# Attention and gated MLP on one core: new measured costs in the instruction planner, and a new table of keys

## The chip, the cores and the metric

The kernel runs on 1 core of one Trainium2 chip. The metric is the device time in microseconds, the median of three runs. Short names: PE is TensorE (its matmuls; PEld its weight loads), DVE is VectorE, ACT is ScalarE, POOL is GpSimd, SP is SyncE, which issues all loads and stores.

## The reference, cut to what matters

q, k and v are 8 batches x 8 heads x 576 positions x 64. Heads 0 to 3 attend locally (a band of 32 positions), heads 4 to 7 along a stride of 32. The result x (576 x 512 a batch) goes through a gated MLP.

```python
scores = scale * np.matmul(q, k.transpose(0, 1, 3, 2))
mask_local = (rel >= 0) & (rel < stride)
mask_strided = (rel >= 0) & (pos[None, :] % stride == pos[:, None] % stride)
scores = np.where(masks[None, :, :, :], scores, -1000000000.0)
attn = np.exp(scores - np.max(scores, axis=-1, keepdims=True))
attn = attn / (np.sum(attn, axis=-1, keepdims=True) + 1e-09)
x = np.matmul(attn, v)                      # heads side by side: 512 wide
h = np.maximum(x @ w_in, 0.0)
u, v = (h[..., :d_ff // 2], h[..., d_ff // 2:])
v_n = (v - mu) / np.sqrt(var + 1e-06)       # over the last axis
v_s = np.einsum('ts,bsd->btd', w_spatial, v_n) + b_spatial[None, :, None]
return ((u * v_s) @ w_out).astype(np.float32)
```

## The kernel before, in words

Everything stays on the chip between the loads and the stores of the result. Each of the 8 batches has four attention tiles of two heads: tile t is `t % 4`, 0 and 1 local, 2 and 3 strided. An attention tile is: loads of q, k and v on SP; scores on PE (L494 local, 36 instructions, L637 strided, 32; each counts as two matmul records); for the first four tiles masks added by PE (L468) and a maximum on DVE (L514, L522, L662); exponentials on ACT (L551, L674); normalising (L447, L451, L456, L668) and a transposition (L575 local, L691 strided) on DVE into the single tile pc; copies of pc to ptl or pts by ACT and POOL (L399, L401); values on PE (L604 local, two halves, L708 strided) into two po buffers; and the split of each half into two fp32r parts, x: a cast on ACT (L421), which frees nothing yet, and the rest, po minus the cast, on DVE (L409), which frees the po buffer. Scores and values use small tiles of the array: 64x32, 128x32, 128x64 and 64x64 instead of 128x128.

The MLP uses full tiles, three fp32r products for each fp32 one: the v half (L969, 512 columns) and the u half (L1026, 288 columns) of w_in, the spatial product (L1107, with its tail L1119 and L1120), and the output projection by 7 block products (L1157), whose operands are split into tile g by a cast (L399 or L401) and a rest (L409). The weights w_in arrive as pairs of 32-bit words, and each of their eight parts is converted at the start by ACT (L789), POOL (L797) and DVE (L805) and then split into two (L399 or L401, L409), as the spatial weights wsp are (loaded in four parts).

All of this is written down as a list of operations, each with a key, the engines that may do it, its cost on each, and what it reads and writes. `Program.order` plans from that list: it goes through time, lets each engine take the ready operation of the lowest key, and gives an operation to another engine if it would end earlier there (`KEYS["dp"]` adds a handicap in ns for DVE, by kind of operation: kind 1 holds the two-input ones). On PE it counts a cost for changing between small-tile (`tiled`) and full-tile operations, and while it is in small tiles it prefers to stay there if the key of the next small tile is near enough. The order of the plan becomes the order of the instructions on each engine, and each engine then works strictly in that order. `KEYS` holds the numbers: "a" the due times of the first eight attention tiles, "lead" how much earlier than needed the later ones are due (10.96 before), "la" and "lb" when q, k and v are fetched, "wv", "wu", "s" and others the weights.

`fillers` looks at the plan: where PE would stand idle for over 700 ns ahead of an operation with a spare buffer (not the masked scores), it puts dummy matmuls of 256 columns there (L1385, `warm`), as many as 0.8 of the gap holds at 427 ns each, so that PE keeps working.

SP keeps at most eight loads under way: each load waits for the one eight places ahead of it. Buffers: two for q, two for k, two for v, two for po, one for pc.

## Time and profile before

| | us |
|---|---|
| runs | 508.29, 508.70, 509.73 |
| median | 508.70 |
| span of the profiled execution | 508.2 |
| PE busy in it | 495.6 |
| DVE, ACT, POOL busy | 345.7, 280.1, 111.4 |

The page gives the span of the profiled execution, from its first to its last instruction, as 508.2 us; the fastest run, 508.29, is the nearest to it. PE is busy for 98% of the span. A slice of 12.7 us near the start is the only one in which it does not reach nine tenths, beside the first and the last. The times of the page are to be read as starts and lengths; consecutive instructions of an engine overlap a little, so the distance between two starts is what an instruction takes of the engine's time.

### The profile page before, as it was taken

Reading aid. Unit: us, or ns where it says so; the run is one execution under the profiler, and the core shown is the slowest. Engines: PE = TensorE matmul, PEld = TensorE weight load, DVE = VectorE, ACT = ScalarE, POOL = GpSimd, SP = SyncE. Lnnn points to the kernel's source line nnn. Section 1 sums busy time; section 2 is a strip of 40 time slices with the busy share of each in tenths; the row PEclk is TensorE's granted clock in tenths of the full one; section 3 lists DMA queues with packets and bytes.
Section 4 is the critical chain, followed back from the end, with each engine's and each line's share of the span. In section 5 each row is a group of like instructions: output and inputs, shape, how many; then the busy total and the mean of one; then the engine's idle time right before and its main releaser. Section 6 shows DMA issues by size and latency. Waiting matters only on the chain.

```text
span 508.2 us, 15732 instructions
## 1 busy us (share of the span) xinstructions
PE 495.6 (98%) x6398; PEld 455.0 (90%) x6398; DVE 345.7 (68%) x1069; ACT 280.1 (55%) x871; POOL 111.4 (22%) x229
## 2 busy tenths in 40 slices
PE   7599999999999999999999999999999999999997
PEld 4478898889988999899998999989998899989997
DVE  3888898988678628784489935687288841666055
ACT  5797777677546566373644764355554642235214
POOL 3554325233232013120221211121022300120000
PEclk9599999999999999999999999999999999999999
DMA  8996442422423312305234243024231020002002
GB/s 288 402 342 233 124 149 98 137 93 56 152 90 121 126 50 91 86 26 153 81 92 138 72 135 91 2 90 135 63 99 44 0 95 0 1 2 93 1 1 94
DMA packets 26103, 52.69 MB, mean 104 GB/s; under 512 B 3120, under 2 KB 11440, under 8 KB 26032
## 3 DMA queue, kind: packets, MB, share of 16 engines
q1 hardware_dynamic: 26032, 51.70, 30.6%
q8 instruction: 50, 0.82, 0.7%
q14 instruction: 21, 0.17, 0.1%
HBM read 42.25 MB, written 9.44 MB: 102 GB/s over the span
## 4 chain that ended last, share of the span: by engine, by line
PE 93%; DMA 4%; DVE 1%; POOL 1%; SPq 0%; issue 0%; ACT 0%; POOLq 0%
PE m L1026 20%; PE m L1107 20%; PE m L969 20%; PE m L1157 18%; PE po L604 3%; PE po L708 3%; PE s L494 2%; PE s L637 2%; PE m L1119 2%; PE m L1120 2%; DMA vn<-w_in 2%; DMA x<-wsp 1%; DMA x<-wtail 1%; POOL ptl L401 0%; SPq L428 0%; POOL kbd L1321 0%
## 5 line engine op out<-in xcount | busy, mean ns | idle before, releaser
L1107 PE MATMUL m<-wsp_sb,vn 128*128 128x288 f32 x768 | 112.9, 296 | 0.0
L1107 PEld LDWEIGHTS m<-wsp_sb,vn 128*128 128x128 f32 x768 | 105.5, 189 | 0.9
L1026 PE MATMUL m<-x,w_in_sb 128*128 128x288 f32 x768 | 105.3, 297 | 0.0
L1026 PEld LDWEIGHTS m<-x,w_in_sb 128*128 128x128 f32 x768 | 103.0, 188 | 0.6
L969 PE MATMUL m<-w_in_sb,x 128*128 128x512 f32 (+1 forms) x408 | 99.5, 398 | 0.0
L1157 PE MATMUL m<-g,w_out 128*128 128x288 f32 x672 | 92.9, 296 | 0.0
L1157 PEld LDWEIGHTS m<-g,w_out 128*128 128x128 f32 x672 | 89.9, 188 | 1.3
L969 PEld LDWEIGHTS m<-w_in_sb,x 128*128 128x128 f32 (+1 forms) x408 | 74.1, 185 | 18.4
L401 POOL TENSOR_SCALAR ptl<-pc 32x64 f32<-32x64 f32 (+3 forms) x98 | 37.9, 387 | 107.2 <-DVE pc L575 71.5
L924 DVE BATCH_NORM_STATS2 bn<-vv 128x6 f32<-128x512 f32 (+1 forms) x37 | 25.3, 685 | 47.4 <-ACT vv L919 47.0
L399 ACT CAST g<-u 128x288 fp32r<-128x288 f32 x91 | 39.0, 435 | 29.1 <-DVE u L820 12.9
L551 ACT ACTIVATE pl<-pl,ml 128x64 f32<-128x64 f32 (+1 forms) x140 | 47.0, 337 | 7.8 <-DVE ml L531 7.7
L937 POOL TENSOR_TENSOR bn<-bn,sel 128x1 f32<-128x1 f32 (+1 forms) x37 | 21.5, 583 | 129.4 <-DVE bn L932 124.5
L409 DVE TENSOR_TENSOR g<-u,g 128x288 fp32r<-128x288 f32 x98 | 43.6, 459 | 7.6 <-ACT g L399 5.3
L919 ACT ACTIVATE vv<-m 128x512 f32<-128x512 f32 (+1 forms) x37 | 22.0, 596 | 47.2 <-PE m L969 46.9
L1129 DVE TENSOR_TENSOR u<-m,u 128x288 f32<-128x288 f32 x56 | 24.9, 454 | 30.6 <-PE m L1120 30.3
L1040 ACT ACTIVATE u<-m 128x288 f32<-128x288 f32 x56 | 22.9, 409 | 41.1 <-PE m L1026 40.3
L399 ACT COPY ptl<-pc 32x320 f32<-32x320 f32 (+3 forms) x94 | 33.5, 356 | 14.5 <-DVE pc L575 12.7
L421 ACT CAST x<-po 128x288 fp32r<-128x288 f32 x60 | 22.2, 399 | 22.1 <-PE po L604 10.6
L409 DVE TENSOR_TENSOR x<-po,x 128x288 fp32r<-128x288 f32 x64 | 27.3, 447 | 7.9 <-ACT x L421 7.1
L531 DVE CUSTOM_DVE_ANT_0 pl<-s,cst_sb 128x64 f32<-128x64 f32 (+1 forms) x140 | 22.1, 214 | 14.4 <-PE s L494 14.4
L551 ACT ACTIVATION_READ_ACCUMULATOR pl<-pl,ml 128x1 f32 (+1 forms) x140 | 26.4, 188 | 0.0
(128 smaller groups left out, 634.1 us busy)
## 6 DMA issues: line engine op xcount, KB each, us to landing
q<-qT SPq DMA_DIRECT2D x32, 295.0 KB, 4.1
v_raw<-vs SPq DMA_DIRECT2D x15, 512.0 KB, 3.7
v_raw<-vl SPq DMA_DIRECT2D x16, 384.0 KB, 3.5
k<-kT SPq DMA_DIRECT2D x16, 304.0 KB, 4.6
kbd<-ks SPq DMA_DIRECT2D x32, 144.0 KB, 4.8
outT<-o SPq DMA_DIRECT2D x32, 144.0 KB, 1.9
outT<-u SPq DMA_DIRECT2D x28, 144.0 KB, 1.8
vn<-w_in SPq DMA_DIRECT2D x4, 512.0 KB, 7.6
```

The lines of the kernel that those rows point to most:

```text
L399: eng.copy(dst(), src())
L401: eng.tensor_scalar(dst(), src(), 1.0, 0.0, op0=ALU.mult, op1=ALU.add)
L409: eng.tensor_tensor(dst(), src(), f32(hi()), op=ALU.subtract)
L421: eng.copy(dst(), src())
L551: eng.activation(p_sb()[:m, u, :], src, AF.Exp, bias=st()[:m, u : u + 1], scale=SCALE if masked else -1.0, **total,)
L924: lambda eng: eng.bn_stats(bn()[:m, 0:6], v()[:m]), [(v,)], [(bn,)],
L969: eng.matmul(v_ps()[:m, :], x_at(kt)[:, a, :], w_in_sb[:, w, kt, HF:], start=(n == 0 and i == 0), stop=(n == NT - 1 and i == 2),)
L1026: eng.matmul(u_ps()[:, :HS], w_in_sb[:, w, kt, f * P : (f + 1) * P], xs[NHP * b + kt]()[:, a, r], start=(n == 0 and i == 0), stop=(n == NT ...
L1040: lambda eng, u=u, f=f, u_ps=u_ps: eng.activation(flat(u)[:, f * HS : (f + 1) * HS], u_ps()[:, :HS], AF.Relu),
L1107: eng.matmul(s_ps()[:, :HS], vn()[:, a, kt, fs], wsp_sb[:, w, kt, r], start=(kt == 0 and i == 0), stop=False,)
L1129: lambda eng, ug=ug, s_ps=s_ps: eng.tensor_tensor(ug(), s_ps()[:, :HS], ug(), op=ALU.mult),
L1157: eng.matmul(o_ps()[:, :HS], w_out_t[0]()[:, w, r, BLOCKS[name], j * P : (j + 1) * P], at(a), start=(first and r == 0 and i == 0), stop=(r ...
```

## The change

The costs that the planner has for the four kinds of small tiles are replaced: local scores 936 to 905 ns, local values 588 to 585, strided scores 784 to 704, strided values 804 to 1066. The change between tile modes costs 88 ns on going into small tiles and nothing on leaving, where it was 45 ns each way. All of `KEYS` is new. The subtraction of "lead" moves from the list `when` to `due`, with the same result. The computation is the same.

```diff
-    "a": (-4467.57, -3072.23, -4097.95, -922.09, -62.58, 1948.86, -54.07, 1313.94,),
+    "a": (-14649.79, -11958.25, -12798.64, -3418.29, -1034.09, 2748.73, 22.98, 2612.65,),
...
-    "lead": (10.96,),
+    "lead": (6.61,),
...
-    "dp": (1410.82, -7913.25, 17481.82, 35293.8,),
+    "dp": (1728.09, 229.43, 40803.9, 48991.77,),
...
-                cost += 45.0 * ((n in self.tiled) != mode)
+                cost += 88.0 * (n in self.tiled and not mode)
...
-            due - 14, [(PE, 26 * 2 * S // STRIDE)], f_s, [(q,), *kin], [(p,) for p in s_ps],
+            due - 14, [(PE, 905)], f_s, [(q,), *kin], [(p,) for p in s_ps],
...
-                due - 1.5, [(PE, 6 * 98)], f_v, [*vin, *ptok], [(o_ps,)],
+                due - 1.5, [(PE, 585)], f_v, [*vin, *ptok], [(o_ps,)],
...
-            due - 14, [(PE, SB * 98)], f_s, [(q,), *kin], [(s_ps,)],
+            due - 14, [(PE, 704)], f_s, [(q,), *kin], [(s_ps,)],
...
-            due - 1.5, [(PE, 4 * SB * 22 + 100)], f_v,
+            due - 1.5, [(PE, 1066)], f_v,
...
-    when = [w - KEYS["lead"][0] for w in when]
...
-        return float(np.interp(t + 1, units, when))
+        return float(np.interp(t + 1, units, when)) - KEYS["lead"][0]
```

**The first values, on SP.** In the first 25 us SP loads the first tiles and the weights; q_2 is the query of tile 1, v_raw_0 the values of tile 0, vn, u and g here staging for w_in. Before:

```order
L428 DMA x_0_178<-wsp 128x576
L428 DMA v_raw_0_180<-vl 128x768
L428 DMA k_2_183<-kT 128x608
L428 DMA q_2_188<-qT 128x590
L428 DMA vn_0_101<-w_in 128x1024
L428 DMA xt_0_228<-vs 128x1024
L428 DMA vn_0_101<-w_in 128x1024
L428 DMA q_3_237<-qT 128x590
```

and after:

```order
L428 DMA q_2_186<-qT 128x590
L428 DMA g_1_188<-w_in 128x1024
L428 DMA x_0_180<-wsp 128x576
L428 DMA k_2_199<-kT 128x608
L428 DMA vn_0_97<-w_in 128x1024 x2
L428 DMA u_1_240<-w_in 128x1024
L428 DMA v_raw_0_243<-vl 128x768
L428 DMA q_3_250<-qT 128x590
```

The values of tile 0 stood two loads ahead of that query, as the 14th load, and now stand seven behind it, as the 22nd; the values of tile 2 (xt) moved ahead.

**The first values, on PE,** from the last scores of tile 1 (m_1, m_2) to the first work on x of tile 0 (x_3) or the values of tile 2 (po_2). Before:

```order
L494 MATMUL m_2_136<-k_1_106,q_2_188 32x64
L1385 MATMUL po_0_335<-zeros_67 32x256
L604 MATMUL po_0_335<-ptl_72,v_raw_0_180 64x96 x6
L604 MATMUL po_1_347<-ptl_72,v_raw_0_180 64x96 x6
L637 MATMUL m_3_139<-kbd_68,q_3_237 32x36 x32
L969 MATMUL m_4_406<-w_in_sb_62,x_3_354 128x512 x3
L708 MATMUL po_2_420<-pts_71,xt_0_228 64x2x18
```

and after:

```order
L494 MATMUL m_2_133<-k_1_176,q_2_186 32x64
L1384 MATMUL po_0_363<-zeros_67 32x256 x12
L604 MATMUL po_0_363<-ptl_72,v_raw_0_243 64x96 x6
L604 MATMUL po_1_385<-ptl_72,v_raw_0_243 64x96 x6
L637 MATMUL m_3_138<-kbd_68,q_3_250 32x36 x32
L708 MATMUL po_2_440<-pts_71,xt_0_136 64x2x18
```

One filler became twelve, and the values of tile 2 follow the scores of tile 3 without full matmuls between. The three fillers that stood ahead of the values of tile 1 are gone.

**The first x, on ACT:** the casts of x of tile 0 (x_3, from po_0 and po_1) and of tile 2 (x_5). Before:

```order
L421 CAST x_3_354<-po_0_335 128x288
L399 COPY pts_71<-pc_1_345 32x16x18
L421 CAST x_3_354<-po_1_347 128x288
L399 COPY pts_71<-pc_1_345 32x16x18
L551 ACTIVATE pl1_76,ml1_78<-m_1_133,ml1_78 128x64 x2
```

and after:

```order
L421 CAST x_3_392<-po_0_363 128x288
L789 ACTIVATE vn_0_97<-vn_0_97 128x512
L421 CAST x_3_392<-po_1_385 128x288
L789 ACTIVATE u_1_240<-u_1_240 128x512
L789 ACTIVATE vn_0_97<-vn_0_97 128x512
L789 ACTIVATE u_0_256<-u_0_256 128x512
L399 CAST w_in_sb_62<-w_out_0_191 128x512
L399 CAST wsp_sb_63<-x_1_128 128x576
L421 CAST x_5_494<-po_2_440 128x18x16
L421 CAST x_5_494<-po_3_442 128x18x16
```

Before, the exponentials of tile 1 (L551) came behind the casts of x of tile 0; now they stand ahead of them, and conversions of w_in stand around them.

**The steady part, on PE:** the end of the strided values of batch 2 and 3's tiles in the output projection, and what follows. Before:

```order
L708 MATMUL po_22_2127<-pts_71,v_raw_10_1878 64x2x18
L708 MATMUL po_23_2129<-pts_71,v_raw_10_1878 64x2x18
L1157 MATMUL m_44_2166<-g_7_1667,w_out_1_1208 128x288 x6
L494 MATMUL s_16_2180<-k_7_1473,q_13_1628 32x64
L494 MATMUL s_17_2182<-k_7_1473,q_13_1628 32x64
```

and after:

```order
L708 MATMUL po_28_2779<-pts_71,v_raw_13_2503 64x2x18
L708 MATMUL po_29_2781<-pts_71,v_raw_13_2503 64x2x18
L494 MATMUL s_20_2816<-k_8_2100,q_16_2512 32x64
L494 MATMUL s_21_2818<-k_8_2100,q_16_2512 32x64
```

Local scores now follow strided values directly. In the whole program POOL has 27 wide two-input operations that DVE had (fifteen of them L409 into g), where it had none.

## Rows read from the trace of the kernel before

**Rows 1.** The page, busy us, share and instructions of each engine.

```profile
PE 495.6 (98%) x6398; PEld 455.0 (90%) x6398; DVE 345.7 (68%) x1069; ACT 280.1 (55%) x871; POOL 111.4 (22%) x229
```

**Rows 2.** Waits of PE: line, for whom, us in total, times, longest.

```profile
PE m L494 <- DMA q<-qT: 7.3, 1, 7.3
```

**Rows 3.** Timeline of PE, start: start us, us, line, tiles, count.

```profile
17.76 1.34 PE L494 MATMUL m<-k,q 64*32 64x64 f32 x72 [7.28 <-DMA q<-qT]
19.03 1.06 PE L1385 MATMUL po<-zeros 128*32 128x256 f32 x2
20.02 2.19 PE L604 MATMUL po<-ptl,v_raw 128*64 128x96 f32 x24
...
30.65 1.48 PE L1385 MATMUL po<-zeros 128*32 128x256 f32 x6
...
43.77 2.40 PE L1026 MATMUL m<-x,w_in_sb 128*128 128x288 f32 x16
```

**Rows 4.** Windows: busy us of PE, PEld, DVE, ACT, POOL; PEclk, DMA, GB/s.

```profile
14.00:17.70 3.70, 0.00 (x0) 0.00 (x0) 3.67 (x10) 2.31 (x5) 0.63 (x1) 0.50 1.03 412
...
22.40:23.40 1.00, 0.95 (x65) 0.93 (x65) 0.71 (x3) 0.95 (x4) 0.30 (x1) 0.70 1.00 385
```

**Rows 5.** Chain of waits in order of time: start us, us, what.

```profile
466.17 12.81 PE m L1026 x96
```

**Rows 6.** Timeline of PE, one small-tile run in the steady part.

```profile
172.77 3.46 PE L1026 MATMUL m<-x,w_in_sb 128*128 128x288 f32 x24
176.16 0.97 PE L494 MATMUL s<-k,q 64*32 64x64 f32 x72
177.06 9.86 PE L1026 MATMUL m<-x,w_in_sb 128*128 128x288 f32 x72
```

**Rows 7.** Timeline of PE, scores followed by strided values.

```profile
54.43 0.97 PE L494 MATMUL s<-k,q 64*32 64x64 f32 x72
55.33 1.14 PE L708 MATMUL po<-pts,v_raw 64*64 64x36 f32 x64
56.40 0.67 PE L1107 MATMUL m<-wsp_sb,vn 128*128 128x288 f32 x3
```

**Rows 8.** Timeline of PE, scores followed by local values.

```profile
253.96 0.97 PE L494 MATMUL s<-k,q 64*32 64x64 f32 x72
255.00 1.21 PE L604 MATMUL po<-ptl,v_raw 128*64 128x96 f32 x24
```

**Rows 9.** DMA issues of 0 to 45 us: count, KB each, us to landing.

```profile
vn<-w_in SPq DMA_DIRECT2D x4, 512.0 KB, 7.6
...
k<-kT SPq DMA_DIRECT2D x5, 304.0 KB, 5.9
x<-wsp SPq DMA_DIRECT2D x4, 288.0 KB, 6.0
v_raw<-vl SPq DMA_DIRECT2D x3, 384.0 KB, 6.3
...
v_raw<-vs SPq DMA_DIRECT2D x2, 512.0 KB, 6.4
```

**Rows 10.** Timeline of DVE, the transposition of tile 0.

```profile
16.05 0.84 DVE L575 STREAM_TRANSPOSE pc<-pl 128x640 f32<-128x640 f32 x1
```

**Rows 11.** Timeline of ACT, exponentials and conversions.

```profile
23.13 0.31 ACT L551 ACTIVATE pl<-m,ml 128x64 f32<-128x64 f32 x1
...
23.44 0.30 ACT L551 ACTIVATE pl<-m,ml 128x64 f32<-128x64 f32 x1
...
27.52 1.27 ACT L789 ACTIVATE vn<-vn 128x512 f32<-128x512 f32 x2
```

**Rows 12.** Groups by line: count, busy us, mean ns, idle before.

```profile
L399 ACT CAST g<-u 128x288 fp32r<-128x288 f32 x91 | 39.0, 435 | 29.1 <-DVE u L820 12.9 <-PE m L1157 9.0 <-DVE u L1129 6.2
...
L409 DVE TENSOR_TENSOR g<-u,g 128x288 fp32r<-128x288 f32 x98 | 43.6, 459 | 7.6 <-ACT g L399 5.3 <-POOL g L401 1.6
...
L937 POOL TENSOR_TENSOR bn<-bn,sel 128x1 f32<-128x1 f32 x35 | 20.2, 580 | 127.0 <-DVE bn L932 122.1 <-DVE mx L447 4.6
```

More of the change, by code (lines that the diff above doesn't have):

```diff
@@ L41 @@
 KEYS = {
-    "a": (-4467.57, -3072.23, -4097.95, -922.09, -62.58, 1948.86, -54.07, 1313.94,),
-    "v": (-1905.33, 2566.85, -1420.01, -351.81,),
-    "u": (2077.2, 2507.69, 3441.61, -704.54,),
-    "s": (1600.35, 689.49, 1605.62, -2112.6,),
-    "t": (-863.37,),
-    "o": (2205.96, 3994.67,),
-    "cst": (-3153.23,),
-    "wv": (1302.43, 874.44, 1384.1, 1780.19,),
-    "wu": (-954.94, -624.77, 1601.45, 150.66,),
-    "lead": (10.96,),
-    "fill": (634.17, 3536.74, 3759.85, 2050.78, 1027.03, 2069.52,),
-    "dp": (1410.82, -7913.25, 17481.82, 35293.8,),
-    "dpt": (1128.82,),
-    "lv": (-2407.03, -1707.29, -454.82, -254.06,),
-    "lu": (1673.71, 2694.32, 1173.88, 457.25,),
-    "lo": (1682.63, -1711.68, 1604.3, -4779.41,),
-    "ls": (-1419.42, 1216.18, -2053.61, -239.17, 1173.72,),
-    "pre": (2.84, 55.65,),
-    "near": (3261.26,),
-    "la": (-2830.09, -2292.21, -5019.65, -1683.98, -4639.4, -3037.2, 298.54, 1600.86,),
-    "lb": (-1002.76, 2105.75, -428.93, 3194.59, 1811.71, 608.19, -588.14, 3548.95,),
+    "a": (-14649.79, -11958.25, -12798.64, -3418.29, -1034.09, 2748.73, 22.98, 2612.65,),
+    "v": (-22602.5, 6765.54, -8978.5, -1009.27,),
+    "u": (2367.68, 7294.49, 15422.81, -3910.53,),
+    "s": (-4960.75, 6447.03, 1975.51, -2850.99,),
+    "t": (4169.61,),
+    "o": (6420.48, 4905.57,),
+    "cst": (-18605.91,),
+    "wv": (-10511.21, 5483.29, 3403.4, 6505.43,),
+    "wu": (-9777.03, -3418.83, -23222.67, -13352.74,),
+    "lead": (6.61,),
+    "fill": (-111.87, -23268.25, 2046.76, 6691.07, 8137.16, 4548.1,),
+    "dp": (1728.09, 229.43, 40803.9, 48991.77,),
+    "dpt": (851.78,),
+    "lv": (-14534.89, -3579.81, 1404.73, 2180.56,),
+    "lu": (6013.7, 2025.88, -1513.91, 642.23,),
+    "lo": (-3714.37, -10376.18, -2778.64, 8993.78,),
+    "ls": (173.79, -1538.13, -11602.57, 6377.62, 9181.26,),
+    "pre": (613.77, 115.61,),
+    "near": (2869.93,),
+    "la": (-16408.92, -3917.39, -12219.84, -21804.11, 269.75, 2221.5, 6904.22, -9719.24,),
+    "lb": (2044.18, 8466.94, -9665.47, -7048.9, 9318.9, 2167.76, -770.9, 5322.07,),
 }
```

## The prediction

> **What bounds the kernel now.** I read the page's busy times first: PE works 495.6 of 508.2 us [rows 1]. So time can be won or lost only in the 12 us or so in which PE has nothing to do, in PE work that computes nothing, and in the price of changing between small and full tiles. The waits of PE then show one long one, 7.3 us for a query tile [rows 2]. The timeline of PE shows what lies around it [rows 3]: the wait ends at 17.76 with the scores of attention tile 1, then come one filler, the values of tile 0 from 20.02, and three more fillers from 30.65. Behind these PE never waits again, and at 43.77 it starts the first u block, with the 48 v matmuls of batch 0 (L969) done. I use that moment as the mark between the start and the steady part. The windows show PE's granted clock at 0.50 (the 1.2 GHz level) while it waits and at 0.70 on average from 22.4 to 23.4 [rows 4]: it fell after PE had stopped, and a mean of 0.70 between 0.50 and 1.00 puts its rise near 23.0, some 5.2 us after PE resumed.
>
> **The price of a small-tile run.** 96 matmuls of 288 columns without interruption take 12.81 us, 0.1334 each [rows 5]. The 24 between two small-tile runs start at 172.77 and are followed at 176.16, after 3.39 us [rows 6], where 24 x 0.1334 is 3.20. So a run costs 0.19 us beside its own tiles. Where two small tiles stand next to each other, the second pays nothing: scores at 54.43, values at 55.33, a full matmul at 56.40, that is 0.90 and 1.07 [rows 7]; alone, the scores take 0.90 too (176.16 to 177.06 [rows 6]). Counted in the order of the programs there are 43 runs before and 34 after, since the strided values (L708) now stand directly ahead of local scores (L494) in ten places. Behind the mark there are 36 against 29, so the gain there is 7 x 0.19 = 1.3 us. The other two runs lie in the start, which is worked out by itself.
>
> In one place a join was dearer: scores at 253.96, values at 255.00 [rows 8], 1.04 instead of 0.90. Values followed by scores are not in the trace. The bounds for each of the ten are 0 and 0.14, for all 0 to 1.4 us; I take 0, by rows 7, which hold the same two kinds of tile in the other order. The Trainium skill (TensorEngine Tiling (Array Packing), Key Properties) says that changing the tiling mode drains TensorE. Rows 7 don't show a drain between two small-tile modes; if there were one at half a run's price, ten joins would give back 0.9 us (estimate).
>
> **The new start: the DMA queue.** While the queue is full it moves 412 GB/s, 402 KB a us [rows 4], and I take loads to land in the order of their issue. Ahead of the query tile of attention tile 1, SP now issues one k (304 KB) and the values of tile 0 (384 KB) less, and one strided value tile (512 KB) more [rows 9]: 176 KB less, 0.4 us, so these scores start at 17.3 instead of 17.76. The values of tile 0 come seven loads behind that query: four of w_in (512 each), one wsp (288), one k (304) and they themselves (384), together 3024 KB or 7.5 us. They land at 24.8. Before, their matmuls ran at 20.02 already.
>
> **The new start: PE.** Twelve fillers now stand between. The scores take 1.27 us at the low clock (17.76 to 19.03 [rows 3]), so they end at 18.6. A filler at full clock takes 0.43 (1.48 for three with the end of the last [rows 3], 0.216 a record), at the low clock 0.86. With the clock rising 5.2 us after 17.3, at 22.5, some 4.6 of them run low and 7.4 at full clock: 18.6 + 3.9 + 3.2 = 25.7. That is 0.9 behind the landing. The values of tile 0 run from 25.7 to 26.8, and their first half is done at 26.3.
>
> **The new start: ACT and DVE, which could be late next.** The transposed weights of tile 0 are there at 16.9 [rows 10]; what DVE does ahead of them hardly changes. Then ACT has, by the spacing of its instructions, which overlap a little (exponentials 0.30 apart, two conversions 1.27 [rows 11]): six copies to ptl 2.2, two casts 1.2, two conversions 1.2, two copies 0.8, ten exponentials 2.9, one cast 0.6. That is 8.9, with 0.3 of waiting 26.1. So the first cast of x for tile 0 comes at 26.5, set by PE; the second, behind a conversion, ends at 27.8, its rest on DVE at 28.3, and PE can read it at 28.5. Until then PE has only 0.7 of scores (tile 3), and then stands still for about 0.9 us, since the values of tile 2 need the two po buffers that the halves of tile 0 hold. They run from 28.5 to 29.6, and the 12 matmuls on x of tile 0 until 32.4.
>
> Meanwhile ACT does three conversions and two casts ahead of the casts of tile 2: 27.8 + 2.9 + 0.7 = 31.4. DVE has eight instructions of 3.1 us ahead of its rests. So x of tile 2 is ready at 32.3, hidden by 0.1 us and no more. From there I find each operand ready about when PE comes to it, and PE's own work counts: 6 matmuls 1.4, scores 1.0, values 1.1, 6 matmuls 1.5, 6 more 1.4, values 1.1, scores 0.7, 6 matmuls 1.5, scores 0.8, and 0.2 of changes: 43.1. With the last 12 matmuls (2.8) the mark is reached at 45.9 instead of 43.77: 2.1 us later.
>
> **The rest.** POOL now does 27 wide two-input operations that all stood on DVE, fifteen of them rests of the output projection. The trace has none of these on POOL; the nearest rows are a two-input one of one column at 0.58 us and DVE's rest of 288 columns at 0.46 [rows 12]. I bound one by 0.58 and 1.2 us and take no cost: an operand half is free and needed again 18 matmuls later, 2.4 us, where a cast of 0.44 [rows 12] and a rest of 1.2 leave 0.8 for the waits between engines. If that cover is gone, each costs PE 0.1 to 0.2, 1.5 to 3 us for fifteen. A gain is open as well, since DVE, busy for 346 us [rows 1], is relieved of some 12; but PE doesn't wait for DVE there, so none is taken. The Trainium skill (SBUF — State Buffer, SBUF: two separate sides) says that a DVE operation with two SBUF inputs and a GpSimd operation that reads SBUF exclude each other for the whole instruction. It speaks against this move; no row here separates it, and it would lengthen DVE, for which no step above waits. The planner's new costs and the moved subtraction of "lead" act only through the order.
>
> **The sum.** 508.2 + 2.1 - 1.3 = 509.0 for the profiled execution; the median of the runs, 508.7, lies 0.5 above its span. Forecast **509.5**.
>
> **Rivals.**
> *ACT and DVE fall behind (slower).* By lengths instead of spacings (0.64 to 0.7 a conversion, rests that meet a POOL operation longer), the second x of tile 0 comes at 29.0 and x of tile 2 at 33.3, 1.0 late; the x of the next two tiles come 0.6 and 0.8 late. The mark is then at 48.3, +4.5, net +3.2: **511.9**. For it: both queues are full in this stretch, and x of tile 2 has 0.1 us of room. Against: the rows follow each other by the shorter spacing. It decides where x of tile 2 comes later than 32.4. Chance 0.26.
> *The start costs nothing (faster).* If the bytes in flight make loads land earlier, the fillers end at 24.4; if the wait for po also goes and every x comes in time, the start is even or a little better and the joins count: 508.7 - 1.3 - 0.4 = **507.0**. Against: ACT's copies and exponentials stand ahead whatever lands. Chance 0.15.
> *The joins are not free:* ten at 0.09 to 0.14 give **510.6**. Chance 0.08.
> *POOL's rests are late in the projection:* **511.5**, by the 1.5 to 3 us above. Chance 0.05.
> *The change does nothing that can be seen,* the fillers taking only idle time and the joins being lost in the start: 508.7. That is within the forecast, whose chance is 0.46.
>
> **Chances and range.** A difference under about 0.3% can't be told from none here, so faster means below 507.2 and slower above 510.2. Faster gets most of the second rival, 0.14; slower gets the first, most of the joins and POOL and the upper end of the forecast, 0.34; same 0.52. The range, 507.0 to 512.0, reaches both main rivals and leaves about 0.2 out.
>
> **What would show it.** Right, if the values of tile 0 (L604) start at about 25.7 behind 12 fillers, PE pauses for about 0.9 us ahead of the first L708, the first L1026 starts near 45.9, and L494 follows L708 after 1.07. Wrong, if x of tile 2 makes PE wait (first rival), if L604 starts near 22, if a join takes longer, or if PE waits anywhere behind the mark.

## The result, and the profile after

The changed kernel is slower. In the first comparison it took 514.91 us (513.42 to 515.95, four runs) against 509.03 for the kernel before, a ratio of 1.0113 with an interval of 1.0090 to 1.0136; in a second one 514.18 against 509.71, 1.0084 (1.0065 to 1.0104). The forecast was 509.5 in a range of 507.0 to 512.0, so it missed by 2 to 3 us beyond the range's end, and the sign had a chance of 0.34.

One number of the sum has to be put right first. In all runs of the two kernels whose span was recorded, the time lies 1.8 to 2.2 us above the span. The kernel before has spans of 506.3 to 508.5 (46 runs, median 507.5); so its first trace, with 508.2, belongs to one of its slower executions, and the 0.5 us by which I went from span to median was wrong. The changed kernel has spans of 510.2 to 513.8 (ten runs, median 512.2). In spans the change costs 4.7 us, where I had 0.8.

The page of the profiled execution of the changed kernel (span 511.5), its first row: busy us, share and instructions.

```profile
PE 497.5 (97%) x6414; PEld 456.5 (89%) x6414; DVE 336.8 (66%) x1037; ACT 282.8 (55%) x874; POOL 130.4 (26%) x258
```

Beside [rows 1], POOL has 29 instructions and 19 us more and DVE 9 us less, as planned. The waits of PE, which answer to [rows 2]:

```profile
PE m L494 <- DMA q<-qT: 6.0, 1, 6.0
PE m L637 <- DMA kbd<-ks: 1.2, 1, 1.2
PE s L494 <- issue: 1.2, 3, 0.6
PE po L708 <- issue: 1.1, 1, 1.1
```

The rows for kbd and for "issue" are new. The first lies at 9.8 us, ahead of the wait for the query, which is long enough to take it in. "Issue" means that PE waited for nothing that the profile shows: once ahead of the first strided values, and three times in local scores. The timeline of the start, which answers to [rows 3]:

```profile
16.62 1.32 PE L494 MATMUL m<-k,q 64*32 64x64 f32 x72 [6.03 <-DMA q<-qT]
17.88 7.17 PE L1384 MATMUL po<-zeros 128*32 128x256 f32 x24
24.98 1.21 PE L604 MATMUL po<-ptl,v_raw 128*64 128x96 f32 x24
26.12 0.77 PE L637 MATMUL m<-kbd,q 128*32 128x36 f32 x64
28.02 1.54 PE L708 MATMUL po<-pts,xt 64*64 64x36 f32 x64 [1.13 <-issue]
...
46.05 3.36 PE L1026 MATMUL m<-x,w_in_sb 128*128 128x288 f32 x24
```

Here the start went nearly as worked out: values of tile 0 at 24.98 (25.7 forecast), a pause of 1.13 (0.9), and at 46.05 (45.9) the first u block, the mark between the start and the steady part. The loss that I did not see is behind the mark, at three places of which this is the timeline:

```profile
121.23 1.14 PE L708 MATMUL po<-pts,v_raw 64*64 64x36 f32 x64
122.30 0.95 PE L494 MATMUL s<-k,q 64*32 64x64 f32 x70
123.58 0.30 PE L494 MATMUL s<-k,q 64*32 64x64 f32 x2 [0.33 <-issue]
...
235.22 0.31 PE L494 MATMUL s<-k,q 64*32 64x64 f32 x5 [0.56 <-issue]
...
291.40 0.33 PE L494 MATMUL s<-k,q 64*32 64x64 f32 x11 [0.28 <-issue]
```

The scores follow the strided values after 1.07 us, as forecast, and then break off with 2, 5 and 11 of their 72 matmuls still to come. By the distance of the starts, a matmul that follows after 0.01 us elsewhere came after 0.54, 0.77 and 0.49: 1.77 us in all. It is one operation that breaks off, at a different matmul each time, which speaks against a wait for data; the next section tests it.

With the two first traces the account closes (starts of matmuls, us):

| | before | after | difference | forecast |
|---|---|---|---|---|
| start, to the first u block | 43.77 | 46.05 | +2.28 | +2.1 |
| going into and out of small tiles behind it, 36 and 29 runs | 7.07 | 5.66 | -1.41 | -1.3 |
| pauses inside local scores | 0 | 1.77 | +1.77 | 0 |
| the rest of PE up to its last matmul | | | +0.61 | 0 |
| behind the last matmul | | | +0.02 | 0 |
| span | 508.2 | 511.5 | +3.3 | +0.8 |

Some of the other executions are slower still in the start, as the next section shows.

### The profile page after: what moved, and what is told of

It is laid out like the page before. It is cut to its first block, busy times and chain, and to the rows that moved or that the text cites. A ratio compares the mean times of both kernels' runs of the same rounds, so it can differ in the third digit from the quotient of the medians.

```text
span 511.5 us, 15737 instructions
## 1 busy us (share of the span) xinstructions
PE 497.5 (97%) x6414; PEld 456.5 (89%) x6414; DVE 336.8 (66%) x1037; ACT 282.8 (55%) x874; POOL 130.4 (26%) x258
## 4 chain that ended last, share of the span: by engine, by line
PE 93%; DMA 5%; issue 0%; SPq 0%; DVE 0%; ACT 0%
PE m L969 21%; PE m L1026 20%; PE m L1107 20%; PE m L1157 18%; PE po L604 3%; PE po L708 3%; DMA vn<-w_in 3%; PE s L494 3%; PE s L637 2%; PE m L1119 2%; PE m L1120 2%; DMA kbd<-ks 1%; DMA k<-kT 1%; SPq L428 0%; DVE x L409 0%
## 5 line engine op out<-in xcount | busy, mean ns | idle before, releaser
L1129 DVE TENSOR_TENSOR u<-m,u 128x288 f32<-128x288 f32 x56 | 24.6, 453 | 46.1 <-PE m L1120 45.9
L401 POOL TENSOR_SCALAR ptl<-pc 32x320 f32<-32x320 f32 (+3 forms) x101 | 36.9, 365 | 68.5 <-DVE pc L575 37.5
L551 ACT ACTIVATE pl<-pl,ml 128x64 f32<-128x64 f32 (+1 forms) x140 | 47.1, 339 | 7.6 <-DVE ml L531 7.4
L409 DVE TENSOR_TENSOR g<-u,g 128x288 fp32r<-128x288 f32 x87 | 39.3, 461 | 6.4 <-ACT g L399 5.8
L409 DVE TENSOR_TENSOR x<-po,x 128x288 fp32r<-128x288 f32 x64 | 26.7, 448 | 21.7 <-ACT x L421 21.4
L399 ACT COPY ptl<-pc 32x320 f32<-32x320 f32 (+3 forms) x91 | 32.3, 355 | 6.5 <-DVE pc L575 4.7
L944 DVE TENSOR_SCALAR vv<-vv,bn 128x512 f32<-128x512 f32 (+1 forms) x37 | 20.1, 543 | 12.9 <-POOL bn L937 12.6
L551 ACT ACTIVATION_READ_ACCUMULATOR pl<-pl,ml 128x1 f32 (+1 forms) x140 | 26.5, 190 | 0.0
## 6 DMA issues: line engine op xcount, KB each, us to landing
v_raw<-vs SPq DMA_DIRECT2D x15, 512.0 KB, 4.4
vn<-w_in SPq DMA_DIRECT2D x4, 512.0 KB, 8.6
```

Of the source, the lines that this page charges most:

```text
L399: eng.copy(dst(), src())
L401: eng.tensor_scalar(dst(), src(), 1.0, 0.0, op0=ALU.mult, op1=ALU.add)
L409: eng.tensor_tensor(dst(), src(), f32(hi()), op=ALU.subtract)
L551: eng.activation(p_sb()[:m, u, :], src, AF.Exp, bias=st()[:m, u : u + 1], scale=SCALE if masked else -1.0, **total,)
L1129: lambda eng, ug=ug, s_ps=s_ps: eng.tensor_tensor(ug(), s_ps()[:, :HS], ug(), op=ALU.mult),
```

## The experiments

**The pauses: blocks of instructions.** The trace has a second kind of transfer beside the loads. The page's row of the instruction queue, and the same row for 120.9 to 122.4 us alone:

```profile
q8 instruction: 50, 0.82, 0.7%
...
q8 instruction: 1, 0.02, 5.2%
```

The trace has 12,963 instructions of PE, weight loads and semaphore instructions included, so about 259 for each of the fifty transfers of 16 KB. In the order of the queue the three matmuls behind the pauses stand 3073 and 1534 places apart, 12 and 6 times 256 to within two places: each is the first of a block of 256, or next to it. The records of the three transfers: 121.04 to 122.29, 232.36 to 233.79 and 289.13 to 290.09; the matmul behind the pause starts 1.29, 1.42 and 1.31 us after their ends. A join of strided values and local scores is 136 matmuls with their weight loads, 272 instructions in 1.97 us. So the theory: PE runs through a block sooner than the next one arrives.

The Trainium skill (Runtime: NRT & Kernel Launch, Instruction fetch mechanics) describes such a supply in blocks of 16 KB or 256 instructions, fetched while the block before is executed, and calls the cost of a border mostly hidden. The trace agrees on the size; at these borders the cost was 0.5 to 0.8 us.

The planner has a guard against this, which I had not described. In `Program.order`, `stock` counts small tiles: 100 at most (`FETCHED`), less those of each operation, plus one for every 32 ns of PE time. After strided values (64) the old cost left 100 - 64 + (804 + 45)/32 = 62.5, too few for the 72 of local scores. The new cost leaves 100 - 64 + (1066 + 88)/32 = 72.06. The measured durations opened the guard by a hair.

First the changed kernel again.

> The changed kernel once more, unaltered. In its first trace PE (TensorE) paused inside three runs of local scores (L494) that follow strided values (L708) directly: 0.53 us at 123.58, 0.76 at 235.22 and 0.48 at 291.40, each 1.3 to 1.4 us behind the end of a 16 KB transfer on the instruction queue (queue 8). Theory (instruction supply): PE's instructions arrive in blocks of 256, and a join of strided values and local scores, 272 instructions in 1.97 us, can use up a block sooner than the next one comes; the places are fixed by the count of instructions, so the same three joins pause again, by 0.3 to 1.5 us each, and nowhere else. Rival (data): the pauses come from what the other engines or the loads do there in that execution; they move or vanish. Time expected 514 to 515 us against about 509 for the kernel before, the spans of both some 2 us below their times.

Measured: 514.18 us, spans 510.2 to 513.7; profiled was the slowest, 513.7. Two of the three joins paused at the same borders, 0.70 us at 126.22 and 0.71 at 237.90; at the third the block came in time (its first matmul 1.94 us behind the transfer's end), and there was one pause more, of 0.29 at 45.40, at a border ahead of the mark. So the expectation held for the places of two, and not in "the same three and nowhere else": a border at a fast stretch can pause, and need not.

Then the borders were moved and nothing else: dummies where PE waits for a query anyway.

```diff
         for _, n, e in issued:
...
+            if n == early:
+                tiny(self.spare[first][1], TINY)
...
+    def tiny(buf, count):
+        for _ in range(count):
+            nc.tensor.matmul(buf()[:STRIDE, :STRIDE], zeros, zeros, start=True, stop=True)
```

> The changed kernel with 37 dummy matmuls of 32 columns (148 instructions with their weight loads) added to PE's queue ahead of the scores of attention tile 1, where PE waits 6 us for a query; every order is the same. All block borders of the instruction supply move 148 instructions earlier in the program. By the first trace the shortest time in which PE then goes through a block is 2.87 us (it was 1.7, 1.7 and 2.05 at the three pauses). Theory (instruction supply): no pause inside a run of scores, so the stretch from the first u block (L1026) to the last matmul, 462.0 us in the first trace of the changed kernel, becomes 460.2 us, and the time falls by 1.8 us or more. Rival (data): the pauses stay near 123, 235 and 291 and the stretch stays at 462. The dummies themselves may move the start by some tenths of a us either way.

> As the kernel shifted by 148, but with 30 dummies (120 instructions). Theory (instruction supply): the three old pauses are gone, and new ones come where the borders now fall: in the joins near 169 and 353 us (a block gone through in 1.66 us by the first trace), 0.3 to 0.8 us each, perhaps one near 39.5 (2.3 us, where the border lies at the start of strided values); so the stretch from the first u block to the last matmul is about 461.2 us. Rival (data): pauses near 123, 235 and 291 as before, none at 169 and 353.

The timeline of PE in the kernel shifted by 120, at an old place and at the two new ones (its lines are 6 higher: L714 is the strided values, L500 the local scores):

```profile
122.14 1.14 PE L714 MATMUL po<-pts,v_raw 64*64 64x36 f32 x64
123.21 0.97 PE L500 MATMUL s<-k,q 64*32 64x64 f32 x72
124.11 1.06 PE L1163 MATMUL m<-g,w_out 128*128 128x288 f32 x6
...
170.07 0.89 PE L500 MATMUL s<-k,q 64*32 64x64 f32 x68
171.41 0.30 PE L500 MATMUL s<-k,q 64*32 64x64 f32 x4 [0.44 <-issue]
...
354.65 0.89 PE L500 MATMUL s<-k,q 64*32 64x64 f32 x68
355.85 0.30 PE L500 MATMUL s<-k,q 64*32 64x64 f32 x4 [0.30 <-issue]
```

The join at 122 runs through, and the joins at 170 and 354 break off, where the count put the borders. The same order of work pauses elsewhere when the instructions are counted differently: the rival falls. Shifted by 148, one pause of 0.32 us is left behind the mark (at 357.0) instead of 1.77, and the stretch from the first u block to the end of the last matmul is 460.65 us, where the changed kernel has 462.04 and 461.83. That is a gain of 1.4 and 1.2 where 1.8 was expected. The times, 515.11 and 514.37, did not fall, since the start came later: the mark is at 49.08 (148) and 46.95 (120). In the kernel shifted by 120, borders fall into v matmuls ahead of the mark, with pauses of 1.2 and 1.6 us. In the one shifted by 148, PE paused for 2.40 us ahead of the first strided values, as in the slower executions shown below, and for 0.6 at a border; its longest pause at a border, 3.6 us among the dummies, fell into the wait for the query and cost nothing (scores at 16.46). I had only allowed some tenths for the start.

In the 17 traces of this study, with 836 blocks, no first matmul of a block starts earlier than 1.22 us after the end of its transfer; where PE paused for a block, the block started 1.2 to 1.6 us after it, whatever stood there. A transfer itself took 0.88 to 2.46 us.

**No joins.** One number of the guard.

```diff
-FETCHED, FETCH_COST = 100.0, 32.0
+FETCHED, FETCH_COST = 99.0, 32.0
```

> The changed kernel with one number of the planner changed: FETCHED 99 instead of 100. The planner keeps a stock of small tiles that may follow each other; strided values take 64 of it and give back 1154/32 = 36.06 in their time, so that 72.06 are left of 100, just enough for the 72 of local scores; with the old costs (804 + 45) 62.5 were left and the join was not allowed. With 99 the ten direct joins are gone again; the program is the same up to the first of them, so the start is the same. Theory (instruction supply, and the run price of 0.19 us from the prediction): 44 runs of small tiles instead of 34, so ten more at 0.19, 1.9 us dearer, and three pauses of 1.8 us in all less: the time within 0.5 us of the changed kernel's first trace, and below its median if the joins pause longer in other executions. Rival (the joins are as dear as single runs or the loss lies in the start alone): 2 us slower, or no difference.

```profile
120.59 1.14 PE L708 MATMUL po<-pts,v_raw 64*64 64x36 f32 x64
121.65 5.82 PE L1157 MATMUL m<-g,w_out 128*128 128x288 f32 x42
```

With 99 the joins are gone (PE's timeline at the first of them), and with them every pause at a border behind the mark. Ten more runs behind it (39) cost 1.94 us at their ends, 0.19 each: the price of the prediction holds. The profiled span is 511.6 beside 511.5, as expected. The median of the times is not: 516.87, with two runs at 513.8 and four at 516.7 to 517.8. What the four lost comes below.

**The start, and why executions differ.** The changed kernel's second trace reached the first u block at 48.52, not 46.05. The program is the same; up to there the largest differences are the length of one pause and the clock. PE's timeline in that trace:

```profile
28.69 1.84 PE L708 MATMUL po<-pts,xt 64*64 64x36 f32 x64 [2.23 <-issue]
...
48.52 1.75 PE L1026 MATMUL m<-x,w_in_sb 128*128 128x288 f32 x12
```

and its granted clock (column PEclk, the third from the end), from 28 us in steps of two:

```profile
28.00:30.00 2.00, 1.17 (x55) 1.12 (x59) 2.00 (x8) 1.39 (x3) 0.73 (x1) 0.94 1.04 407
30.00:32.00 2.00, 2.00 (x23) 1.64 (x18) 2.00 (x5) 1.80 (x5) 1.58 (x1) 0.50 1.04 402
32.00:34.00 2.00, 2.00 (x8) 1.59 (x7) 2.00 (x6) 1.87 (x6) 1.71 (x3) 0.71 1.02 392
```

PE had paused for 2.23 us up to 28.69; the clock fell to its lower level (1.2 GHz) at about 29.7 and came back at about 33.2, with PE busy. In the first trace the pause was 1.13 and the clock stayed at 1.00. So I tried both ends of this: a shorter pause, and a filled one.

The pause: the first strided values need the po buffers, and these come free with the rests of x of tile 0 on DVE. I had the second cast on ACT set their time. The timelines of DVE and POOL say otherwise (rest of w_in, then the two rests of x; POOL's conversion):

```profile
26.39 1.17 DVE L409 TENSOR_TENSOR w_in_sb<-w_out,w_in_sb 128x512 fp32r<-128x512 f32 x1
27.48 0.81 DVE L409 TENSOR_TENSOR x<-po,x 128x288 fp32r<-128x288 f32 x2
...
26.20 0.82 POOL L797 TENSOR_SCALAR vn<-vn 128x512 int32<-128x512 uint8 x1 [0.34 <-DMA vn<-w_in]
```

and in the kernel without joins, whose start is the same program:

```profile
26.09 0.68 DVE L409 TENSOR_TENSOR w_in_sb<-w_out,w_in_sb 128x512 fp32r<-128x512 f32 x1
26.69 0.81 DVE L409 TENSOR_TENSOR x<-po,x 128x288 fp32r<-128x288 f32 x2
...
26.70 0.67 POOL L797 TENSOR_SCALAR vn<-vn 128x512 int32<-128x512 uint8 x1 [1.13 <-DMA vn<-w_in]
```

The rests of x stand behind a rest of w_in. Beside POOL's conversion that took 1.17 us; where POOL stood waiting for a load it took 0.68 (and began 0.3 us earlier), and PE's pause was 0.57 instead of 1.13. The Trainium skill (SBUF — State Buffer, SBUF: two separate sides) has a two-input DVE operation and a GpSimd operation that reads SBUF exclude each other, and these rows agree. In the prediction I set that rule aside because no step waited for DVE; here one did.

```diff
+        for late, behind in ((156, 79), (146, 78)):
+            op = issued.pop(place(late))
+            issued.insert(place(behind) + 1, op)
```

> The changed kernel with two instructions put back in their queues: on DVE the rest of a part of w_in (L409 into w_in_sb) stands behind the two rests of x of tile 0 instead of ahead of them, and on ACT one conversion (L789) behind the second cast of x instead of ahead of it. PE's order is the same. In the traces of the changed kernel PE stands still for 1.13 and 2.23 us ahead of the first strided values (L708); they start 0.5 us behind the start of the first of these two rests, and the rests follow a chain of POOL, DVE, ACT and DVE work on w_in that starts when that part has landed. Theory (order on DVE): the rests come at about 26.3 and 26.9 instead of 27.5 and 27.9, PE waits 0.3 us or less, and the first u block starts 0.7 to 1.5 us earlier; where PE's clock fell after the long pause (to 0.50 from 29.9 to 33.1 in the second trace of the changed kernel, which cost some 1.6 us more) it doesn't fall. So the time falls by 1 to 2 us, to 512 to 513. Rival (PE is bound by something else there, the next casts or loads): no difference, since the wait moves behind.

Measured: 513.71 us, spans 510.1 to 512.8. The expectation failed in size: the rests came at 27.00, half a us earlier and not 1.2, since the chain on w_in ahead of them began 0.55 us later in this execution (its first DVE instruction, L809 here, at 24.13; L805 in the changed kernel at 23.58); the pause was 1.13 again in the trace, and the clock fell (0.50 from 30 to 32). Against 514.18 nothing is shown.

```diff
+            if n == 98:
+                warm(self.spare[348][1], 4)
```

> The changed kernel with four more dummy matmuls of 256 columns (8 records, 0.86 us at full clock) ahead of the first strided values (L708), written to the buffer of the first v block, which is free; nothing else moves, but all block borders of the instruction supply move by 16 instructions. Theory (clock): PE's pause there is shorter by up to 0.86 us, its start of L708 is as before where the pause was over 0.86, and the granted clock stays at 1.00 behind it also in executions with a long pause; so the slowest executions (515.8 of 512.2 to 515.8) go, the spread narrows to 1.5 us, and the median falls by 0.5 to 1 us. Rival (the spread has another cause): the spread stays at 3 us and the clock falls in the trace as it did. In the joins, by the passage times of the first trace (1.89 and 2.27 us) two pauses near 123 and 235 remain.

Its windows of the clock, to be set beside those of the second trace above:

```profile
28.00:30.00 2.00, 1.16 (x62) 1.11 (x64) 2.00 (x8) 1.43 (x3) 0.75 (x1) 1.00 1.05 413
30.00:32.00 2.00, 2.00 (x25) 1.64 (x18) 2.00 (x5) 1.82 (x5) 1.59 (x1) 1.00 1.04 423
```

The strided values started at 28.70, as late as in the second trace, and yet the clock stayed at 1.00 and the mark came at 46.70 instead of 48.52, as the clock theory has it. The times are 512.04 to 513.81, median 513.19: the slowest executions are gone, though the spread, 1.8 us, stayed over the 1.5 expected. The fall of the median, 1.0 us, is not shown to be the clock's: the dummies also moved the borders by 16 instructions, the pauses behind the mark are 0.51 and 0.31 us (at 124.06 and 235.19), and the stretch to the last matmul is 460.87 us, 1.0 to 1.2 shorter than in the changed kernel.

Then three of the losses together: that order on DVE and ACT, six narrow dummies in the pause, and through these a shift by 24 instructions.

```diff
+            if n == 98:
+                warm(self.spare[348][1], 6, 128)
```

> The changed kernel with three of its losses taken away together: the rests of x of tile 0 ahead of a rest of w_in on DVE (and its second cast ahead of a conversion on ACT), as in the run of that alone; six dummy matmuls of 128 columns (0.65 us) ahead of the first strided values, so that PE's clock doesn't fall; and these move the block borders by 24 instructions, by which the passages that paused take 2.4, 2.5 and 2.8 us instead of 1.7, 1.7 and 2.05. Theory: first u block at 45.2 to 46.5, clock at 1.00 throughout, pauses of 0.4 us at most in all, so a span of 509.3 to 510.5 and a time of 511.3 to 512.5 with a spread under 1.5 us; what then remains over the kernel before (509.7) is the later values of tile 0, 2 to 3 us, less 0.8 of fewer runs. Rival (the losses don't add, as another wait comes behind): 513 or more, as each alone gave 513.2 and 513.7.

PE's timeline in it (L714 strided values, L1032 u):

```profile
27.57 1.54 PE L714 MATMUL po<-pts,xt 64*64 64x36 f32 x64 [0.16 <-issue]
...
46.11 3.34 PE L1032 MATMUL m<-x,w_in_sb 128*128 128x288 f32 x24
```

512.09 us, all five runs within 511.90 to 512.25, spans 509.8 to 510.2: as expected, 2.1 below the changed kernel, with nearly none of its spread. One pause of 0.29 us is left behind the mark, and the stretch to the last matmul is 460.57 us, 0.5 shorter than before and 1.3 to 1.5 shorter than in the changed kernel; so by the traces most of the 2.1 us is the pauses. What still stands against the kernel before, 2.6 us, is the start: 46.11 against 43.77 and 42.72 in its two traces.

**What makes the start late: the load, or the orders on ACT and DVE.** One load moved, in the kernel before to where the changed kernel has it, and in the changed kernel to behind the query of tile 1 (there with `fillers[74] = 4` too):

```diff
+        op = issued.pop(place(34))
+        issued.insert(place(174) + 1, op)
```

> The kernel before with one load moved: the values of tile 0, the 14th load, are issued behind the eight loads that follow the query of tile 1 (2.9 MB, as in the changed kernel), and nothing else. Theory (the late values are what makes the new start late): they land at about 24 us, PE stands idle at the low clock from 19 to 24, and the casts and rests of x of tile 0 stand ahead of all else on ACT and DVE, so the first u block comes at 46.5 to 48.5 instead of 42.7 to 43.8, and the time is 513 to 515. Rival (ACT's and DVE's own work sets the start, whatever lands): first u block within 1 us of that before, 510 to 511.

> The changed kernel with that load moved the other way: the values of tile 0 are issued right behind the query of tile 1, ahead of the six loads of w_in and others, and the twelve fillers ahead of their matmuls become four; the orders on ACT, DVE and POOL stay. Theory (in the changed kernel ACT's and DVE's orders bind as tightly as the load): the values run at about 20.5, but the casts of x of tile 0 stand behind ten exponentials on ACT, which end at 25.5 to 26, so the strided values (L708) start at 27 to 28.7 as before and the first u block at 45.5 to 48.5; PE stands idle for over 5 us ahead of them, so the clock is more often low behind it: time 513 to 516, no better. Rival (the load alone holds it): first u block at 43 to 44, time 510.5 to 511.5. The eight fillers less move the block borders by 32 instructions; by the trace one passage of 1.65 us near 180 and one of 2.5 near 289 pause.

PE's timelines at the values of tile 0, of the kernel before with the late load (L607, L711, L1029 are the values, the strided values and u):

```profile
24.46 2.19 PE L607 MATMUL po<-ptl,v_raw 128*64 128x96 f32 x24 [6.84 <-DMA v_raw<-vl]
...
28.48 1.14 PE L711 MATMUL po<-pts,xt 64*64 64x36 f32 x64
...
48.01 2.27 PE L1029 MATMUL m<-x,w_in_sb 128*128 128x288 f32 x15
```

and of the changed kernel with the early one (L608, L712, L1030):

```profile
21.52 1.21 PE L608 MATMUL po<-ptl,v_raw 128*64 128x96 f32 x24
...
27.96 2.35 PE L712 MATMUL po<-pts,xt 64*64 64x36 f32 x64 [1.75 <-POOL vn L801]
...
47.51 2.69 PE L1030 MATMUL m<-x,w_in_sb 128*128 128x288 f32 x19
```

Both came out as expected: 514.71 us for the one, 513.83 for the other. In the kernel before the late load is enough to make the start late (part of it is the clock, which was at 0.50 until 27.4 there, as no fillers stand in that wait), and in the changed kernel taking it away is not enough to mend it: values 3.5 us earlier bring the strided values forward by nothing, since the rests of x stand where they stood (27.41, against 27.48). PE then idles from 22.7 to 25.0 and again for 1.75 us up to 27.96, and its clock is down to 0.50 until about 31.8. The start of the changed kernel hangs on all of its orders together. The two pauses that I expected near 180 and 289 are missing: at 182.22 PE had gone through a block in 1.66 us, as fast as at the pauses of the changed kernel, but the transfer of the next had started 1.24 us ahead of the border before; at the three pauses of the changed kernel it started between 0.44 us ahead of that border and 0.26 behind it.

> The kernel without joins once more, for the trace of a slow execution (four of its six were at 516.7 to 517.8, two at 513.8, and the trace was of one of the two). Theory (clock): a slow one has a longer pause ahead of the first strided values, a granted clock of 0.50 for some us behind it, and the first u block at 48 to 49 instead of 45.41; the stretch behind it is the same 466.2 us to the end. Rival (something behind the mark): the first u block at 45 to 46 and the stretch 3 us longer.

This run took 516.89 us, as the four did. Its first u block comes at 48.45, 3.04 us behind that of the fast one, and the stretch from there to the end is 466.24 us, in the fast one 466.23. PE paused for 2.47 us ahead of the strided values, and the windows of its clock read:

```profile
30.00:32.00 2.00, 2.00 (x29) 1.64 (x22) 2.00 (x5) 1.95 (x5) 1.49 (x1) 0.50 1.06 419
32.00:34.00 2.00, 2.00 (x7) 1.60 (x6) 2.00 (x6) 1.75 (x5) 1.71 (x4) 0.65 1.00 394
```

So the 3 us between these two executions lie in the start, and they go with a long pause and a clock that falls behind it, as between the two traces of the changed kernel (46.05 and 48.52).

**The kernel before again, and with a filled wait.**

> The kernel before once more, for a second trace. In the runs beside the changed kernel its spans were 506.8 to 508.2 us, 2.0 below its times, so its first trace (508.2) is one of its slower executions. Expected: the first u block at 43.0 to 43.8, the steady part 464.4 us as in the first trace, no pause inside a run of small tiles.

Measured: span 507.2, first u block at 42.72 (0.3 ahead of what I expected), the steady part up to the end of the span 464.44, no pause in it. So the start of the kernel before varies too, by about 1 us, and its steady part does not.

```diff
+            if n == early:
+                warm(self.spare[first][1], EARLY)
```

> The kernel before with twelve dummy matmuls of 256 columns (5.2 us at full clock) on PE ahead of the scores of attention tile 1, where PE waits 6.8 to 7.3 us for the query and where the planner puts none, since masked scores have no spare buffer; they write to a po buffer that is still free. No other order changes. Theory (clock): in the kernel before the granted clock falls to 0.50 at 12.8 us, in this wait, and stays there until 23, so the scores, the values of tile 0 and the masked scores of tile 3 run at half speed; with the dummies it stays at 1.00 and PE's work between 16.9 and 23.4 is 1.5 to 2.3 us shorter. The first u block then starts 0.8 to 1.5 us earlier (43.8 and 42.7 in the two traces of before), time 508.2 to 509. Rival (the loads and ACT set the start): no difference, 509.6. A border of the instruction supply moves into the run at 54.5 us (2.37 us by the trace), a pause of 0.3 us at most.

The windows of its clock:

```profile
20.00:22.00 2.00, 0.93 (x68) 0.76 (x68) 2.00 (x7) 1.95 (x6) 1.69 (x4) 1.00 1.05 407
22.00:24.00 2.00, 1.36 (x15) 0.63 (x3) 1.97 (x4) 2.00 (x15) 1.92 (x3) 0.76 1.05 408
24.00:26.00 2.00, 2.00 (x66) 1.88 (x65) 1.74 (x2) 0.56 (x4) 1.76 (x3) 0.50 1.03 412
```

511.86 us, 2.4 slower than before (1.0042, 1.0025 to 1.0060). The clock did stay at 1.00 through the wait, but PE then ran ahead of what it needs: it stood still for 0.73, 1.07 and 0.64 us (for ptl, for x and for a block), the clock fell near 23, and the work from 23.05 to 29.9 ran low. Here the filled wait only moved the idle time.

**Halves of the change.**

> The changed kernel (new planner costs) with the keys of the kernel before for the start (due times of the first eight tiles, fetch times, weights, and the orders within v, u, s, t and o), and the new ones for lead, pre, near and dp alone. The plan has 12 fillers in all as before, the values of tile 0 early, 33 runs of small tiles (43 before), and 11 joins of strided values and local scores, one of them over a block border by the estimate. Theory (the loss is the start, some 2.3 to 4.8 us by the traces, and the block borders, 1.4 to 1.8 us): the start is as in the kernel before, the steady part is that of the changed kernel with one pause instead of three, 464.2 us; span 507.5 to 508.5, time 509.5 to 510.5, as the kernel before. Rival (the loss is in the new steady order): 511.5 or more.

> The new planner costs alone: the changed kernel with all keys of the kernel before. The first 28 loads stand in the order of the kernel before, with the values of tile 0 early (13th); 36 runs of small tiles (43 before, 34 in the changed kernel); joins of strided values with local scores in six places and with strided scores in five. Theory (the loss is in the new start and in block borders): the start is near that of the kernel before; one pause of 0.5 to 0.8 us where a block falls into a run of four tiles near 85 us (1.4 us by the estimate); time 509.5 to 511, within 0.3% of the kernel before. Rival (the joins or the new costs are what costs): 512 or more.

> The new keys alone: the kernel before (old planner costs) with all keys of the changed kernel. The first loads stand as in the changed kernel, with the values of tile 0 seven loads behind the query of tile 1; 16 fillers beside the first eight; 39 runs of small tiles, only two joins of strided values and local scores. Theory: the start is as late as in the changed kernel (first u block at 46 or later) and the gain of joined runs is mostly absent, so 513 to 516, no better than the changed kernel. Rival (the costs, not the keys, carry the loss): about 510.

All three missed: 515.29, 523.79 and 532.77 us. For the last two a part of the reason is in the longest wait of PE behind the mark. Of the new costs alone:

```profile
PE s L494 <- DVE ml L531: 4.2, 1, 4.2
```

and of the new keys alone:

```profile
PE s L494 <- issue: 5.3, 1, 5.3
```

Around these waits the clock fell as well (0.50 from 101.2 to 108.0 us and from 63.0 to 73.2). Each half gives a plan of its own, with waits that neither kernel has, so they say nothing on which half of the change carries the loss; that keys fit only the costs that they were made for is likely from this and not shown. The one with the old start keys does have the steady part expected (464.28 us, one pause of 0.29), but its start is another plan's as well: first u block at 47.40. So its time lies where the rival had it, and not for the rival's reason.

## Why the prediction was right and wrong

**The start, +2.1: right for one kind of execution, too small for the others.** Measured +2.28 between the first traces. The landing of the values (24.13, forecast 24.8), the scores (16.62 against 17.3), the end of the fillers and the pause are each within about 0.7. That the mark is within 0.15 is partly luck: up to the fillers' end all came 0.7 early, and from the strided values to the mark PE took 18.0 us where I had 17.4. The late load is enough for a late start, as the kernel before with that load shows, and ACT and DVE bind as tightly, as worked out. One link was wrong: the rests waited on DVE and not for the cast on ACT, which was there at 27.0. And a start forecast from one trace has the clock of that trace. I had the clock rise 5.2 us after the scores start; it rose after 4.9 in the first trace of the changed kernel and after 2.9 in the second, and that it can fall again behind the pause stands nowhere in my sum. In the second pair of traces the loss is 5.8 us (42.72 to 48.52). My rival of a late ACT and DVE had 48.3 for the mark; its number came, but by a longer pause and a fallen clock.

**The run price, 7 x 0.19: right.** 1.41 us measured at the ends of the runs, 0.19 each in the kernel without joins. The 0.61 that came back elsewhere is spread over the runs of full matmuls; what it is stays open.

**The joins, taken as free: the step that failed.** I bounded each of the ten by two neighbouring rows, 0 and 0.14, and asked only whether PE pays for the change of mode. The rows of the same two tiles in the other order [rows 7] were free because no border lay badly: one falls into them at 54.80, but PE had taken 11.2 us for the block that ends there and took 5.3 for the next. The price is not one of the join. It is paid where a block is run through faster than the next arrives, three of ten in the first trace and two in the second, at 0.5 to 0.8 us. The rival "the joins are not free" named the place without the mechanism; its total, 0.9 to 1.4 us for ten joins, came near the 1.8 and 1.4 us of the two traces by luck, since two or three joins paid it all. A sign was in the trace of before: the last strided scores ahead of the mark, at 42.91, take 0.87 us to the next start, where others take 0.70; a block border falls there, 1.51 us after a transfer. And the planner's guard stood in the code that the diff touches; working out its sum with the new cost would have shown that the change lifts the guard exactly for the joins.

**POOL's two-input operations: right.** PE waits for none of them behind the mark.

**From span to time: wrong by 1.5 us.** I added 0.5 where the runs have about 2.0; as the first trace of the kernel before lay 0.7 above the median of its spans, 0.8 of this stayed in the forecast.

**The whole miss, 509.5 to 514.2.** Of the 4.7 us, 0.8 is that step from span to time. Behind the mark the traces of the two kernels differ by +0.8 to +1.0 us where I had -1.3: some 2.2 us, the pauses and the 0.6 that stays open. What is left of the difference of the median spans puts the start at +3.8 (an estimate, as medians have no trace) where I had +2.1: 1.7 us. By the traces those are the executions in which the clock falls; how many do is not known.

**The range.** Its upper end took each rival alone. A late start and dear joins came together, and both had been given a chance.

**A row read wrongly.** I wrote that behind the fillers at 30.65 PE never waits again; it waited once more, 0.35 us at 32.48, for POOL's copy to ptl. Nothing in the sum rests on it.

## What to carry to other kernels

Where small matmuls stand close together, count instructions, weight loads included, and not only time: the stretches that paused here behind the mark would have gone through their 256 in 1.7 to 2.9 us, and an edit anywhere ahead moves the borders. That speed alone does not decide: the kernel before ran through a block in 2.2 us (265.47 to 267.67) without a pause. A planner that has such a guard should be read for what new numbers do to the guard. And a start should be forecast from two or three traces, since one short pause of TensorE can cost more behind it, through the clock, than by itself.

## What the runs showed of the hardware

- The first matmul of a block starts 1.22 us after the end of its transfer at the earliest. From the start of a transfer to a paused matmul it was 2.2 to 3.2 us in the steady part.
- What starts a transfer stays open. The one that the first pause waited for started at 121.04, 0.28 us before PE passed the border ahead (121.32); the next started at 128.39, 4.8 us after PE had passed its border at 123.58. Where a fast block was not followed by a pause, the transfer had started early: 1.43 us ahead of the border in the kernel before (264.04), 1.24 in the changed kernel with the early load.
- The granted clock fell after PE had resumed: in the second trace of the changed kernel about 1.1 us after a pause of 2.23 us, and in the kernel with the rests of x first 1.9 us after a pause of 1.13, the length with which it did not fall in the first trace. It had been high since 19.5 and 19.2 us there, and since 21.6 in the first trace.
- The rest of a w_in part (128x512, two inputs) took 0.68 us on DVE alone and 1.17 beside a conversion on POOL.
